# First rows, conversion steps and merge places reordered in a delta-rule, gated-MLP and Mish-MLP kernel

## The chip, the cores and the metric

One core of a Trainium2 chip. The metric is the time of one execution on the device in microseconds; the compiled program is fully unrolled, and each engine works through its own queue of instructions in the order in which the program issues them.

## The reference, cut to what matters

```python
B, H, S, D = 4, 8, 768, 48
k_n = k / (norm(k) + 1e-06)
for t in range(S):                                  # delta rule, state 48 x 48 for each of 32 heads
    y[:, :, t] = q_t @ state
    v_old = k_t @ state
    state = state + beta_t * outer(k_t, v_t - v_old)
x = y as 3072 tokens x 384
xn = x / sqrt(mean(x * x) + 1e-06) * rms_g          # first MLP, d_ff 1536
x = (silu(xn @ w_gate) * (xn @ w_val)) @ w_out
h = x @ w_in                                        # second MLP, d_ff 2048
out = (h * tanh(softplus(h))) @ w_out2
```

q, k, v, beta, x are float32; the weights come as float64 and are used as a high and a low part.

## The kernel before

The sequence is cut into 12 rows of 64 tokens, two to a segment. Within a row the delta rule becomes matrix products: the Gram matrix of k is turned into the inverse of a triangular 64 x 64 matrix (tile `A`, called Y when done), then values, outputs and the new state follow. The state goes from row to row, so the rows stand in a chain.

**Phase b1** (to about 482 us) works off the rows. `chain_row(r)` yields the stages of a row in an order written out by hand: `R0` for row 0, `R1` for row 1, `ROW` for the others. A letter is a stage: r residual of v against the state, q0 q1 turns (transposes) of q, p scores (masked Gram matrix), y output of the state, v values, o0 o1 outputs, k update of the state, s0 s1 x0 x1 normalisation and x for the MLP, and for row r+4: nA norm, nB scaling of k (on GpSimd), c0 c1 turns of k, g its Gram matrix. S, T, X, Y are s0, s1, x0, x1 of the row before, done late.

The inverses come in two kinds. `inlane(sg)` inverts all 32 x 32 blocks of a segment's two rows on VectorE (copies of products `pr`, sums, three 32 x 32 transposes, the last of them `yc`, L605), then ScalarE copies into `A` (L607 to L609). `merges(sg)` joins the 32 x 32 blocks of each row to 64 x 64 with TensorE (L621, L631) and ScalarE copies between. For the first two rows `quick_lane(r)` (VectorE, 16 x 16) and `quick_products(r)` (TensorE, L735, then the same merge) stand in. `lanes()` runs `inlane` of segment 2, 3, ... and, once a given share of it is issued, the merges of the segment before.

Beside the chain run: `part_a`, the first MLP for two of its six column pairs (due units by row in `DUE`, for row 1 behind a delay `OFF`); `cv`, the conversion of weights from float64 (`convs`); warm-up matmuls (`warm`). `merge(*streams)` interleaves them: of the (generator, weight) pairs it always takes the next step of the one with the smallest share of its weight done. So a weight says over which stretch of the row a stream's steps are spread, and a stream whose steps sum to more than its weight ends after the others. `PRE` writes out the turns (t), products (g), norms (n), scalings (s), warm-ups (w) and steps of row 0's chain (c) that are issued ahead of the rows.

`convs` takes half a weight tile at a time through: load into `raw` (ring of 4), absolute value into `t` (ring of 3; ScalarE L138, or VectorE L140), two steps of two VectorE instructions (L143, L146; L151, L154), and at last the high part (ScalarE L165, or VectorE L167) and the low part (GpSimd L168). The absolute value of the next half is issued ahead of the steps of this one.

**Phase b2** does the other four pairs of the first MLP, **phase c** the second MLP; both are block after block of matmuls. The last ten halves of `w_out2` (tiles `wqh`, `wql`) are converted at the end of b2 and in the first three batches of c, there with VectorE for every step but the low part.

At the start `setup` issues on SyncE the loads of k for rows 0 to 3, then beta for the quick inverses (`load_bq`, eight small loads for each of the first two row pairs), q, beta again, v, weights. Pools: `il` is closed when row 10 begins and its place is reused for converted weights, `kp` lives to the end of the rows.

Of the kernel before, what the change touches and what calls it, by code (L numbers as in the profile page):

```python
# [8 lines left out]
F32 = mybir.dt.float32  # L9
# [10 lines left out]
P = dict(  # L20
    XB=2, WE=16, RB=4, TB=3, LANE=15.7, XL=1, HH=0, DPRE=5, WU0=24, WU1=35, WARM=[0, 0], CVS=[2.6, 10.0, 2.5, 13.1, 0], CVA=12, CVT=12.22, CVB0=0, CVB1=1.238, CVC=2.31, PSD=1, INV=1, Q=[0, 2.7, 1.2, 9.9, 0, 18.8, 2.8, 3.0, 11.5, 10.6, 11.0, 19.4], W=[22, 2, 14, 8, 0, 14], SQ=5, CVP=0, NE=2, BQ=3, NU=6, CVN=1, CVE=14.671, CVD=4.076, OFF=2.9,
    ROW="r nA q0 q1 S p T y nB X Y v c0 c1 k o0 g o1".split(),
    R0="r q0 q1 p nA v o0 o1 s0 nB k s1 x0 c0 c1 g".split(),
    R1="r nA q0 Y q1 y p nB v k o0 o1 s0 s1 x0 c0 c1 g".split(),
    DUE=[0, 4, 6, 11],
    PRE="t00 t01 w1 g0 s1 n2 w2 s2 t10 | n3 t11 c g1 c c s3 t20 t21 | t30 g2 t31 w3 g3".split(),
    C=dict(n=0.2, q=0.5, r=1.4, y=1.1, p=1.2, v=1.2, o=0.9, k=1.2, s=0.1, x=0.45, c=0.4, d=0.4, g=1.2, h=1.2),
# [40 lines left out]
def kernel(  # L68
# [14 lines left out]
    nc = tc.nc  # L83
# [88 lines left out]
    def convs(pairs, wait=0):  # L172
        depth = P["RB"]
        gens = [g for p in pairs for g in p]
        for g in gens[:depth]:
            next(g)
        yield 0.1
        yield from delay(wait)
        next(gens[0])
        yield 0.2  # L180
        for i, g in enumerate(gens):
            if i + 1 < len(gens):
                next(gens[i + 1])
            for _ in range(2):
                next(g)
                yield 0.7
            if i + depth < len(gens):
                next(gens[i + depth])
            for _ in g:
                pass  # L190
            yield 0.1

    def cols(w, m):
# [82 lines left out]
    def phase_b1():  # L276
# [75 lines left out]
        def setup():  # L352
# [9 lines left out]
            for r in range(4):  # L362
                load_k(r)
                nc.vector.memset(khp[r][:, :, D:64], 0.0)
                if r == P["BQ"]:
                    load_bq(0)
                    load_q(0)
            load_bq(1)
            nc.gpsimd.memset(half, HALF)
# [143 lines left out]
        def inlane(sg):  # L513
# [85 lines left out]
            yield 1.1  # L599
            X11 = il.tile([128, 32, 32], F32, tag="X11", name="X11")  # L600
            nc.vector.transpose(out=X11.rearrange("p u r -> p r u"), in_=Nv.rearrange("p c r -> p r c"))
# [40 lines left out]
        def quick_lane(r):  # L642
# [7 lines left out]
            us = slice(r * 16, r * 16 + 16)  # L650
            compq = il.tile([128, 32, 32], F32, tag="X11", name="compq")
            comp = compq[:, 0:16, :]
# [110 lines left out]
        def merges(sg):  # L763
            X11 = X11_t.pop(sg)
            for rl in range(2):
                us = slice(rl * 16, rl * 16 + 16)
                Z = il.tile([128, 16, 32], F32, tag="Z", name="Z")
                yield from merge32(2 * sg + rl, X11[:, us], Z)

        def lanes():  # L770

            ending = iter(())
            for sg in range(2, NSEG):
                done_of, due = 0.0, 4.0
                for w in inlane(sg):
                    yield w
                    done_of += w
                    if done_of >= due:
                        next(ending, None)
                        due += 2.5  # L780
                for _ in ending:
                    pass
                ending = merges(sg)
            yield from delay(P["INV"])
            yield from ending

# [236 lines left out]
        sq = [flat(t)[:, 0:16 * D].rearrange("p (u d) -> p u d", d=D) for t in sq]  # L1023
        run(warm(W_[0]), norm(0), scale_k(0, nc.vector), norm(1, spare))
        chain0 = chain_row(0)
# [20 lines left out]
        for x in P["PRE"]:  # L1046
            if x == "|" or not PRE:
                PRE.append([])
            if x != "|":
                PRE[-1].append(x)  # L1050
        run(ahead_of(PRE[0]))
        merge((quick_lane(0), 12), (seq(delay(Q[0]), ahead_of(PRE[1])), Q[1] + Q[0]))

        def reset():
# [7 lines left out]
            (first, 7.0),  # L1062
            (quick_lane(1), Q[3]),
            (seq(delay(Q[4]), ahead_of(PRE[2])), Q[4] + Q[5]),
            (budget(cv, Q[6]), Q[7]),
        )
        lane, laned = lanes(), [0.0]
        M1A = 4.0 * FA + KD
        ps_ds = [ps_d]
        part_a = gated((ps_u, ps_ds, hp, tp), range(FA), range(NR), get_xa, finish_a, next_x)  # L1070
        for sg in range(NSEG):
            for rl in range(2):
# [10 lines left out]
                if r == 0:  # L1083
                    lane1 = seq(reset(), inlane(1), delay(P["INV"]), merges(1))
                    streams.append((budget(lane1, Q[8]), Q[8]))
# [3 lines left out]
                elif sg + 1 < NSEG:  # L1089
                    upto = (r - 1) * P["LANE"] if r < NR - 3 else 999.0  # L1090
                    streams.append((until(lane, laned, upto), P["LANE"] + (0.0 if r < NR - 3 else 7.0)))
                elif rl == 0:
                    st_i.close()
                    wbp.append(st_b.enter_context(pool("wbA")))
                    todo = [(c, m, cols(w, m)) for m in range(FA, NP1) for c, w in (("g", w_gate), ("v", w_val))]
# [190 lines left out]
```

## Time and profile before

| | us |
|---|---|
| runs (3) | 1235.88, 1236.47, 1233.67; median 1235.88 |
| the profiled execution | 1236.43 |
| its span, first to last instruction | 1234.7 |
| TensorE busy, matmuls | 1123.7 (91%) |
| VectorE busy | 732.4 (59%) |
| ScalarE busy | 561.9 (46%) |
| GpSimd busy | 438.2 (35%) |

The page shows in 40 slices of some 31 us that TensorE is at 90% and more from slice 17 on but for one dip, and at 40 to 90% before, with a granted clock of 0.6 to 0.8 in the first five slices. A busy share over the whole span therefore says little; the stretches below are read one by one. In these views PE is TensorE, DVE VectorE, ACT ScalarE, POOL GpSimd, SP SyncE; a q behind the name is the engine's own queue (DMA issues). In the order of time, a line gives start, duration, engine, line, operation, output and inputs, and in brackets the idle time before it and who ended it.

### The profile page before, as it was taken

What the parts mean: (1) busy time and instruction counts of PE and PEld (TensorE: products, weight loads), DVE (VectorE), ACT (ScalarE), POOL (GpSimd) and SP (SyncE); (2) the same over time, 40 slices, a digit from 0 to 9 for tenths busy, and PEclk for the clock granted to TensorE, in tenths of its full rate; (3) what the DMA queues carried; (4) which work ended last, traced back from release to release, by engine and by line L of the source; (5) the groups of instructions that cost most, each with busy time, mean ns of one, the idle gap of its engine ahead of it and who ended that gap; (6) DMA issues with size and microseconds to landing.
All of it is one profiled execution on the core that took longest, in us unless ns stands there. A gap on an engine that the chain in (4) does not pass through costs nothing.

```text
span 1234.7 us, 32507 instructions
## 1 busy us (share of the span) xinstructions
PE 1123.7 (91%) x14172; PEld 1092.3 (88%) x14172; DVE 732.4 (59%) x1135; ACT 561.9 (46%) x1064; POOL 438.2 (35%) x392
## 2 busy tenths in 40 slices
PE   6674598999997978999999999988999999999998
PEld 5563587989897868999999999987999999999998
DVE  5768697988886797555555552368434333343333
ACT  3463545656555654211111110154756555565672
POOL 2124244444421354344443442244323232232232
PEclk8667688999998899999999999999999999999999
DMA  6224032332223544333433222331111011111101
GB/s 121 52 67 104 14 79 68 78 84 75 70 77 104 143 142 154 116 103 122 135 115 105 90 82 98 124 103 56 39 39 40 22 31 39 40 40 39 34 7 26
DMA packets 121695, 95.02 MB, mean 77 GB/s; under 512 B 81104, under 2 KB 104144, under 8 KB 121552
## 3 DMA queue, kind: packets, MB, share of 16 engines
q1 hardware_dynamic: 109456, 69.34, 20.6%
q10 hardware_dynamic: 12096, 23.60, 5.7%
q8 instruction: 111, 1.82, 0.6%
q14 instruction: 32, 0.26, 0.1%
HBM read 64.60 MB, written 28.31 MB: 75 GB/s over the span
## 4 chain that ended last, share of the span: by engine, by line
PE 66%; DVE 16%; ACT 5%; issue 3%; POOL 1%; DMA 0%; DVEq 0%; POOLq 0%; ACTq 0%
PE pd L1182 5%; PE pd L1183 5%; PE pd L1181 5%; PE ph L210 5%; PE ph L211 5%; PE ph L212 5%; DVE pr L540 4%; PE pg L210 4%; PE pv L210 3%; PE pd L227 3%; PE pg L211 3%; PE pv L211 3%; PE pv L212 3%; PE pg L212 3%; PE pd L228 3%; PE pd L229 3%
## 5 line engine op out<-in xcount | busy, mean ns | idle before, releaser
L1229 POOL TENSOR_TENSOR gl<-t,gh 128x512 fp32r<-128x512 f32 x96 | 125.3, 1306 | 254.5 <-DVE gh L1228 253.1
L255 POOL TENSOR_TENSOR hl<-sg,hh 128x512 fp32r<-128x512 f32 x72 | 97.2, 1350 | 237.4 <-DVE hh L254 216.9
L210 PE MATMUL ph<-xh,wih 128*128 128x256 f32 x576 | 162.7, 283 | 4.6 <-DVE t L1225 4.6
L211 PE MATMUL ph<-xl,wih 128*128 128x256 f32 x576 | 162.7, 282 | 0.0
L212 PE MATMUL ph<-xh,wil 128*128 128x256 f32 x576 | 162.5, 282 | 0.0
L245 ACT ACTIVATE sg<-pg 128x512 f32<-128x512 f32 x72 | 43.0, 597 | 236.4 <-PE pg L212 206.8
L1181 PE MATMUL pd<-wqh,gh 128*128 128x384 f32 x384 | 130.3, 339 | 1.9 <-DVE wqh L167 1.9
L1182 PE MATMUL pd<-wql,gh 128*128 128x384 f32 x384 | 130.3, 339 | 1.7 <-POOL wql L168 1.7
L1183 PE MATMUL pd<-wqh,gl 128*128 128x384 f32 x384 | 129.9, 338 | 0.0
L211 PE MATMUL pg<-xl,wgh 128*128 128x256 f32 x432 | 124.2, 288 | 5.2 <-POOL xl L933 5.2
L210 PE MATMUL pg<-xh,wgh 128*128 128x256 f32 x432 | 128.3, 297 | 0.0
L210 PE MATMUL pv<-xh,wvh 128*128 128x256 f32 x432 | 127.7, 296 | 0.0
L227 PE MATMUL pd<-hh,woh 128*128 128x256 f32 x432 | 125.1, 290 | 2.2 <-DVE hh L254 1.6
L212 PE MATMUL pg<-xh,wgl 128*128 128x256 f32 x432 | 124.0, 287 | 0.0
L211 PE MATMUL pv<-xl,wvh 128*128 128x256 f32 x432 | 123.9, 287 | 0.0
L212 PE MATMUL pv<-xh,wvl 128*128 128x256 f32 x432 | 123.7, 286 | 0.0
L228 PE MATMUL pd<-hl,woh 128*128 128x256 f32 x432 | 122.4, 283 | 1.0 <-POOL hl L255 1.0
L229 PE MATMUL pd<-hh,wol 128*128 128x256 f32 x432 | 122.1, 283 | 0.0
L251 DVE TENSOR_TENSOR sg<-sg,pv 128x512 f32<-128x512 f32 x72 | 49.3, 685 | 112.9 <-PE pv L212 110.6
L1225 DVE TENSOR_TENSOR t<-t,ph 128x512 f32<-128x512 f32 x96 | 65.2, 680 | 83.5 <-ACT t L1223 83.4
L210 PEld LDWEIGHTS ph<-xh,wih 128*128 128x128 f32 x576 | 109.8, 191 | 4.8 <-DVE t L1225 4.8
L212 PEld LDWEIGHTS ph<-xh,wil 128*128 128x128 f32 x576 | 109.8, 191 | 0.0
(187 smaller groups left out, 2938.5 us busy)
## 6 DMA issues: line engine op xcount, KB each, us to landing
raw<-in_moe_w_out_dram SPq DMA_DIRECT2D x28, 384.0 KB
raw<-in_moe_w_in_dram SPq DMA_DIRECT2D x16, 384.0 KB
kh<-in_k_dram SPq DMA_DIRECT2D x24, 192.0 KB
qp<-in_q_dram SPq DMA_DIRECT2D x24, 192.0 KB
v<-in_v_dram SPq DMA_DIRECT2D x48, 96.0 KB
raw<-in_moe_w_gate_dram SPq DMA_DIRECT2D x12, 384.0 KB
raw<-in_moe_w_val_dram SPq DMA_DIRECT2D x12, 384.0 KB
xh_d<-xh SPq DMA_DIRECT2D x12, 384.0 KB
```

What stands on the lines that cost most here:

```text
L210: nc.tensor.matmul(ps[:, f, :], wh[:, kt, sl], xh[:, kt, :], start=(kt == 0), stop=False)
L211: nc.tensor.matmul(ps[:, f, :], wh[:, kt, sl], xl[:, kt, :], start=False, stop=False)
L212: nc.tensor.matmul(ps[:, f, :], wl[:, kt, sl], xh[:, kt, :], start=False, stop=(kt == KD - 1))
L227: nc.tensor.matmul(ps, wh[:, f, sl], hh[:, f, :], start=(i + f == 0), stop=False)
L228: nc.tensor.matmul(ps, wh[:, f, sl], hl[:, f, :], start=False, stop=False)
L229: nc.tensor.matmul(ps, wl[:, f, sl], hh[:, f, :], start=False, stop=last)
L255: nc.gpsimd.tensor_tensor(out=hl, in0=sg, in1=hh.bitcast(F32), op=ALU.subtract)
L1181: nc.tensor.matmul(ps, gh[:, f, sl], wh[:, f, :], start=(m + f == 0), stop=False)
L1182: nc.tensor.matmul(ps, gh[:, f, sl], wl[:, f, :], start=False, stop=False)
L1183: nc.tensor.matmul(ps, gl[:, f, sl], wh[:, f, :], start=False, stop=last)
L1225: nc.vector.tensor_tensor(out=t, in0=t, in1=ps, op=ALU.mult)
L1229: nc.gpsimd.tensor_tensor(out=gl, in0=t, in1=gh.bitcast(F32), op=ALU.subtract)
```

## The change

- Start: beta for the first pair of rows is loaded second (behind k of row 0), q third, beta again behind k of row 2. The scaling of k for row 1 is issued with its norm, the turns and products of row 0 at once behind it; turns of row 1 and row 0's chain steps beside lane 0, closed by 40 warm-ups; norms and scalings of rows 2 and 3 ahead of lane 1; turns and products of rows 2 and 3 in the later part of that merge.
- Orders: row 0 updates the state ahead of its outputs. From row 2 on nB stands ahead of y, v ahead of Y, k ahead of the turns of row r+4, and g last. Row 1 has 5 units of part_a instead of 4, behind a delay of 6 instead of 2.9; row 2 has 5 instead of 6.
- Merges: those of segment 1 (rows 2 and 3) go from the end of row 1's stream into `lanes`, beside the inverse of segment 2; within an inverse merges start at 2.5 units and follow every 2.0 (4.0 and 2.5 before). The last merges (rows 10 and 11) go from the end of row 9's lane into a stream of their own beside row 10. The lane is held 1.5 units behind.
- Conversions: the last step of a half (high and low part) is issued after the VectorE steps of the next half.
- The tiles `X11` (with `compq`) and `Z` move from pool `il` to `kp`.

```diff
-    ... W=[22, 2, 14, 8, 0, 14], ... OFF=2.9,
-    ROW="r nA q0 q1 S p T y nB X Y v c0 c1 k o0 g o1".split(),
-    R0="r q0 q1 p nA v o0 o1 s0 nB k s1 x0 c0 c1 g".split(),
+    ... W=[22, 40], ... OFF=6.0,
+    ROW="r nA q0 q1 S p T nB y X v Y k c0 o0 c1 o1 g".split(),
+    R0="r q0 q1 p nA v k o0 o1 s0 nB s1 x0 c0 c1 g".split(),
-    DUE=[0, 4, 6, 11],
-    PRE="t00 t01 w1 g0 s1 n2 w2 s2 t10 | n3 t11 c g1 c c s3 t20 t21 | t30 g2 t31 w3 g3".split(),
+    DUE=[0, 5, 5, 11],
+    PRE="t10 t11 c g1 c c w1 | t20 t21 g2 t30 t31 g3".split(),
...
+        last = iter(())
         for i, g in enumerate(gens):
             if i + 1 < len(gens):
                 next(gens[i + 1])
...
             if i + depth < len(gens):
                 next(gens[i + depth])
-            for _ in g:
+            for _ in last:
                 pass
+            last = g
             yield 0.1
+        for _ in last:
+            pass
...
-                if r == P["BQ"]:
+                if r == 0:
                     load_bq(0)
+                elif r == 1:
                     load_q(0)
-            load_bq(1)
+                elif r == 2:
+                    load_bq(1)
...
-            X11 = il.tile([128, 32, 32], F32, tag="X11", name="X11")
+            X11 = kp.tile([128, 32, 32], F32, tag="X11", name="X11")
...
-        def lanes():
-            ending = iter(())
+        def lanes(ending):
             for sg in range(2, NSEG):
-                done_of, due = 0.0, 4.0
+                done_of, due = 0.0, 2.5
...
-                        due += 2.5
+                        due += 2.0
...
-            yield from delay(P["INV"])
-            yield from ending
+            left.append(ending)
...
-        run(warm(W_[0]), norm(0), scale_k(0, nc.vector), norm(1, spare))
+        run(warm(W_[0]), norm(0), scale_k(0, nc.vector), norm(1, spare), scale_k(1))
...
-        run(ahead_of(PRE[0]))
-        merge((quick_lane(0), 12), (seq(delay(Q[0]), ahead_of(PRE[1])), Q[1] + Q[0]))
+        run(turn_k(0, 0), turn_k(0, 1), products(0))
+        merge((quick_lane(0), 12), (ahead_of(PRE[0]), 6.0))
...
             (first, 7.0),
-            (quick_lane(1), Q[3]),
-            (seq(delay(Q[4]), ahead_of(PRE[2])), Q[4] + Q[5]),
+            (seq(*[f(r, *a) for r in (2, 3) for f, a in ((norm, (sq[r - 2],)), (scale_k, ()))], quick_lane(1)), 12.5),
+            (seq(delay(8.0), ahead_of(PRE[1])), 14.0),
             (budget(cv, Q[6]), Q[7]),
...
-        lane, laned = lanes(), [0.0]
+        lane, laned, left = lanes(merges(1)), [0.0], []
...
-                    lane1 = seq(reset(), inlane(1), delay(P["INV"]), merges(1))
+                    lane1 = seq(reset(), inlane(1))
...
-                    upto = (r - 1) * P["LANE"] if r < NR - 3 else 999.0
-                    streams.append((until(lane, laned, upto), P["LANE"] + (0.0 if r < NR - 3 else 7.0)))
+                    upto = (r - 1) * P["LANE"] - 1.5 if r < NR - 3 else 999.0
+                    streams.append((until(lane, laned, upto), P["LANE"]))
                 elif rl == 0:
                     st_i.close()
+                    streams.append((seq(left.pop(), delay(7.0)), 13.0))
```

## Rows read from the trace of the kernel before

**Rows 1.** Busy time by stretch: us, length, busy of each engine, PEclk, DMA share, GB/s.
```profile
92.40:142.60 50.20, 24.21 (x480) 21.27 (x480) 45.92 (x61) 20.85 (x49) 22.95 (x17) 0.74 0.28 72
...
142.60:154.80 12.20, 7.96 (x257) 7.40 (x258) 0.04 (x1) 7.63 (x13) 0.18 (x1) 0.50 0.00 1
...
211.00:389.00 178.00, 167.34 (x3908) 155.81 (x3906) 153.13 (x195) 104.82 (x250) 67.42 (x59) 0.97 0.31 82
...
389.00:405.50 16.50, 12.81 (x291) 11.78 (x291) 1.23 (x4) 10.32 (x18) 2.00 (x3) 0.65 0.10 34
...
405.50:482.00 76.50, 64.41 (x955) 60.76 (x956) 62.71 (x100) 44.64 (x124) 36.94 (x38) 0.92 0.51 155
...
817.00:863.00 46.00, 37.68 (x250) 35.62 (x248) 43.21 (x70) 23.13 (x33) 22.86 (x19) 0.95 0.24 78
```

**Rows 2.** Who waited for whom on VectorE, 0 to 160 us: total, times, longest.
```profile
DVE v L818 <- PE pp L813: 18.9, 2, 12.2
...
DVE qc L646 <- DMA qc<-in_beta_dram: 5.9, 1, 5.9
...
DVE compq L509 <- ACT compq L508: 5.1, 1, 5.1
...
DVE PT L492 <- PE pp L483: 3.5, 1, 3.5
```

**Rows 3.** In order of time: SyncE's first loads and the first reader of k.
```profile
0.79 7.79 SPq L331 DMA_DIRECT2D kh<-in_k_dram  x8
...
5.53 0.84 ACT L423 ACTIVATE sq<-kh 128x768 f32<-128x768 f32 x1 [3.24 <-DMA kh<-in_k_dram]
...
8.63 6.17 SPq L358 DMA_DIRECT2D qc<-in_beta_dram  x8
...
16.25 5.77 SPq L358 DMA_DIRECT2D qc<-in_beta_dram  x8
```

**Rows 4.** In order of time: warm-ups, norm of k3 and lane 0's transpose.
```profile
12.75 3.39 PE L1013 MATMUL warm<-ident 128*128 128x128 f32 x28
...
24.23 0.95 DVE L425 TENSOR_REDUCE ss<-sq 128x16 f32<-128x768 f32 x1
...
26.46 1.04 DVE L659 STREAM_TRANSPOSE dq<-compq 128x512 f32<-128x512 f32 x1
```

**Rows 5.** In order of time: second and third product of row 0's inverse, TensorE.
```profile
41.03 1.54 PE L735 MATMUL pp<-Zq,YT 32*32 32x32 f32 x49 [1.42 <-DVE Zq L740]
...
51.56 1.10 PE L735 MATMUL pp<-YT,Zq 32*32 32x32 f32 x58
```

**Rows 6.** In order of time: end of segment 1's inverse, start of segment 2's.
```profile
139.67 1.92 DVE L605 STREAM_TRANSPOSE yc<-N__166 128x1024 f32<-128x1024 f32 x1
...
143.84 1.04 ACT L609 COPY A<-yc 32x1024 f32<-32x1024 f32 x1
...
155.70 1.28 DVE L509 SCALAR_TENSOR_TENSOR comp<-A,h,comp 128x1024 f32<-128x1024 f32 x1
```

**Rows 7.** Waits of TensorE, 0 to 500 us, and one of ScalarE's, whole span.
```profile
PE pp L502 <- POOL kh L449: 11.1, 4, 4.0
...
PE pp L899 <- ACT ve L855: 1.5, 6, 0.6
...
ACT wgh L165 <- DVE t L154: 15.5, 6, 3.8
```

**Rows 8.** In order of time: conversion steps in the dip, last product at its end.
```profile
824.98 0.35 DVE L140 TENSOR_SCALAR t<-raw 128x384 int32<-128x384 int32 x1
...
825.25 1.18 DVE L143 TENSOR_SCALAR t<-t 128x384 f32<-128x384 f32 x1
...
825.15 1.07 POOL L168 TENSOR_TENSOR wql<-t,wqh 128x384 fp32r<-128x384 f32 x1 [0.89 <-DVE wqh L167]
...
858.73 0.35 DVE L143 TENSOR_SCALAR t<-t 128x384 f32<-128x384 f32 x1
...
862.86 0.69 PE L1182 MATMUL pd<-wql,gh 128*128 128x384 f32 x1 [0.39 <-POOL wql L168]
```

More of the change, by code (lines that the diff above doesn't have):

```diff
@@ L20 @@
 P = dict(
-    XB=2, WE=16, RB=4, TB=3, LANE=15.7, XL=1, HH=0, DPRE=5, WU0=24, WU1=35, WARM=[0, 0], CVS=[2.6, 10.0, 2.5, 13.1, 0], CVA=12, CVT=12.22, CVB0=0, CVB1=1.238, CVC=2.31, PSD=1, INV=1, Q=[0, 2.7, 1.2, 9.9, 0, 18.8, 2.8, 3.0, 11.5, 10.6, 11.0, 19.4], W=[22, 2, 14, 8, 0, 14], SQ=5, CVP=0, NE=2, BQ=3, NU=6, CVN=1, CVE=14.671, CVD=4.076, OFF=2.9,
-    ROW="r nA q0 q1 S p T y nB X Y v c0 c1 k o0 g o1".split(),
-    R0="r q0 q1 p nA v o0 o1 s0 nB k s1 x0 c0 c1 g".split(),
+    XB=2, WE=16, RB=4, TB=3, LANE=15.7, XL=1, HH=0, DPRE=5, WU0=24, WU1=35, WARM=[0, 0], CVS=[2.6, 10.0, 2.5, 13.1, 0], CVA=12, CVT=12.22, CVB0=0, CVB1=1.238, CVC=2.31, PSD=1, INV=1, Q=[0, 2.7, 1.2, 9.9, 0, 18.8, 2.8, 3.0, 11.5, 10.6, 11.0, 19.4], W=[22, 40], SQ=5, CVP=0, NE=2, BQ=3, NU=6, CVN=1, CVE=14.671, CVD=4.076, OFF=6.0,
+    ROW="r nA q0 q1 S p T nB y X v Y k c0 o0 c1 o1 g".split(),
+    R0="r q0 q1 p nA v k o0 o1 s0 nB s1 x0 c0 c1 g".split(),
     R1="r nA q0 Y q1 y p nB v k o0 o1 s0 s1 x0 c0 c1 g".split(),
-    DUE=[0, 4, 6, 11],
-    PRE="t00 t01 w1 g0 s1 n2 w2 s2 t10 | n3 t11 c g1 c c s3 t20 t21 | t30 g2 t31 w3 g3".split(),
+    DUE=[0, 5, 5, 11],
+    PRE="t10 t11 c g1 c c w1 | t20 t21 g2 t30 t31 g3".split(),
     C=dict(n=0.2, q=0.5, r=1.4, y=1.1, p=1.2, v=1.2, o=0.9, k=1.2, s=0.1, x=0.45, c=0.4, d=0.4, g=1.2, h=1.2),
@@ L650, in quick_lane @@
             us = slice(r * 16, r * 16 + 16)
-            compq = il.tile([128, 32, 32], F32, tag="X11", name="compq")
+            compq = kp.tile([128, 32, 32], F32, tag="X11", name="compq")
             comp = compq[:, 0:16, :]
@@ L766, in merges @@
                 us = slice(rl * 16, rl * 16 + 16)
-                Z = il.tile([128, 16, 32], F32, tag="Z", name="Z")
+                Z = kp.tile([128, 16, 32], F32, tag="Z", name="Z")
                 yield from merge32(2 * sg + rl, X11[:, us], Z)
-        def lanes():
-            ending = iter(())
+        def lanes(ending):
             for sg in range(2, NSEG):
-                done_of, due = 0.0, 4.0
+                done_of, due = 0.0, 2.5
                 for w in inlane(sg):
```

## The prediction, made before the change was run

> **What bounds the kernel now.** I read the busy time by stretch first [rows 1], to see which engine is full where. From 482 us on TensorE runs almost without a break but for one dip, 817 to 863. Before 482 us it does not: 92.4 to 142.6 belongs to VectorE (45.92 of 50.2 us busy), 211 to 389 to both (TensorE 167.34 and VectorE 153.13 of 178 us). Two holes stand out: 142.6 to 154.8 (VectorE busy 0.04 us) and 389 to 405.5 (1.23 us). What ends late before 482 shifts all that follows, since the rest is TensorE work one behind the other; so a microsecond taken from the chain of the first stretch is a microsecond of the span, and one added in the dip too. Then I read who waited for whom on VectorE in the first 160 us [rows 2], and the order of time around each of those waits [rows 3 to 6].
>
> **Beta second.** The first 16-step inverse on VectorE waits 5.9 us for beta [rows 2]. SyncE issues eight loads of k in 7.79 us (0.97 each), eight beta loads in 6.17 and, after q, the last eight in 5.77, ending at 22.02 [rows 3]. The change puts one eight behind k0 and leaves only k3 (two issues, 1.9 us) behind the second. Beta comes 1.9 us sooner. k1 is moved behind the first eight: it is issued at 0.79 + 1.9 + 6.2 = 8.9 and, by the 4.7 us that k0 took from its issue to its reader at 5.53 [rows 3], arrives at 13.6. Its norm stands on ScalarE ahead of row 0's copies; with some 5 us for the norm (passes of 0.84 and 0.95 in [rows 3, 4]), copies and products these end near 18.5: later than before, but ahead of beta, whose issue alone ends at 22.02 - 1.9 = 20.1, so beta stays last.
> The Trainium skill speaks against this term: "DMA: Bandwidth & Descriptors", "Issuing engines are not separate DMA queues", calls a sequencer's issue time usually small relative to the DMA itself. Here it is not: 16 loads of 1 KB hold SyncE for 11.9 us [rows 3]. By the page the 1.9 us would be 0, and the time about 1217.
> The norm of k3, from 24.23 on VectorE, holds the transpose that starts the lane until 26.46 [rows 4]; put behind lane 0 it frees 2.2 us. Together 4.1 us at the end of lane 0. What is late next is TensorE: 40 warm-up matmuls now stand behind row 0's scores and ahead of the first product; at 0.12 us each (28 in 3.39 [rows 4]) 4.8 us, and double that at the lower clock level, which may take all 4.1 back. The two norms now ahead of lane 1 fall into the 5.1 us in which VectorE waited for compq [rows 2]. I take **-3.4**, between 0 and -4.1.
>
> **Row 0's products ahead of the turns.** The second product starts at 41.03, the third, which needs nothing newer than the second's operands, at 51.56 [rows 5]: between them TensorE's queue holds two turns, row 2's and row 3's products and warm-ups. In the new merge these start at 8 of 14, so row 0's inverse can end several us sooner, and its values, and row 1's inverse behind them. VectorE gains only where it waits: 18.9 - 12.2 = 6.7 us for row 1's residual and 3.5 us for row 1's scores [rows 2]. The second is TensorE standing in block 0's products ahead of the scores; their delay goes from 2 of 6.9 to 6 of 11 of the row, past the scores. Bounds 0 and -10.2; I take half, **-5**, because GpSimd's and ScalarE's queues hold both chains too.
>
> **Row 1 to row 2.** The inverse of rows 2 and 3 ends on VectorE at 139.67 + 1.92, its copies on ScalarE at 143.84 + 1.04 = 144.88 [rows 6]. Then both merges run, with nothing beside them, and only then row 2's residual and the next inverse, whose first VectorE step is at 155.70 [rows 6]. With the merges handed to the lane stream, that step needs only the copies and the diagonal on ScalarE, a pass as long as the last copy and taken at its 1.04: 145.9, so 9.8 us sooner. The merges do not vanish: this hole holds 7.96 us of TensorE at granted clock 0.50 [rows 1], 4.0 us at full speed, now inside row 2. If all of it lay on the path 5.8 would be left. Row 2 has 5 units of block work where later rows have 11, which leaves room: **-8**, bounds -5.8 and -9.8.
>
> **Rows 2 to 9, new order.** TensorE's largest wait is for GpSimd's scaled k, 11.1 us in four waits up to 4.0 [rows 7]. nB moves ahead of y and the turns behind Y and k, some three of a row's 12 cost units, so this wait should go. What comes instead: the state update now directly follows the values and their four ScalarE copies; that wait's longest is 0.6 now [rows 7], times eight rows +5. The moved nB puts a VectorE reciprocal sooner in its queue, behind it the inverse, and it may wait for GpSimd's power. TensorE idles only 10.7 us in the 178 [rows 1]: **-2**, between -8 and +5.
>
> **Row 9 to row 10.** The same hole, 16.5 us, with TensorE busy 12.81 at clock 0.65 [rows 1]: 8.3 us at full speed, so 8.2 can go. The last merges now run beside row 10's residual, turns and block work, and row 10's conversions find VectorE 10 us sooner. The merges' ping-pong with ScalarE still stands ahead of row 10's values: **-6**, bounds -2 and -8.2.
>
> **Conversions a half later.** ScalarE's cast no longer waits for VectorE (one tile's row of four: 15.5 us [rows 7]), but the next half's first step now follows at once on the low part that GpSimd has just been given, since three t tiles serve in a ring. In rows 10 and 11 the one against the other: **-1**, between -4 and +4 of the 12.1 us that TensorE idles there [rows 1].
> In the dip it costs. There the conversions run on VectorE alone, 43.21 of 46 us busy [rows 1], and the last product waits for the last low part at 862.86 [rows 8]. Now L143 of the next half takes 1.18 beside L168 and 0.35 alone [rows 8]: VectorE already loses 0.83 a half to GpSimd, ending at 826.43. After, L140 starts when L168 is done (826.22 + 0.1), then L140 and L143 at 0.35 each, ends overlapping by 0.1: 826.9. That is 0.5 for each of the seven halves that reuse a tile, 3.5; at the end two low parts come back to back, 1.07 [rows 8] and 0.3: **+4.9**. Behind the waiting L140 stand the half's four steps and the next batch's multiply, for which TensorE waits. Bounds: +1.4 (the end alone) and 7 x 1.25 + 1.4 = +10.2, if L143 stays at 1.18.
> The Trainium skill ("SBUF — State Buffer", "SBUF: two separate sides") has VectorE and GpSimd lock each other out for a whole instruction. By it the 0.83 is a wait for that same low part and is not paid twice, as the 0.35 row has it; were it no lock, the dip would cost the +10.2 and the time be 1221.
> The tiles moved to the longer-lived pool are the same instructions on other addresses: 0, as long as no new tile waits for theirs.
>
> **The sum.** -3.4 - 5 - 8 - 2 - 6 - 1 + 4.9 = -20.5. The profiled execution took 1236.43 (span 1234.7), 0.55 above the median of the runs, 1235.88: 1215.4, so 1215.
>
> **Rivals.**
> *The holes only move* (15%): row 2's and row 10's values wait for their merges as before, the queues in order stand still behind them, and the -8 and -6 go, -2 with them. Left: -3.4 - 5 - 1 + 4.9 = -4.5, 1231. For it: values stand in the middle of the row, the merges just before. Against: VectorE's next inverse needs no merge.
> *More than the sum* (12%): VectorE keeps full from lane 1 on (-10.2 for the -5) and the waits for scaled k go (-8): -32, 1204. For it: all these waits are on full engines. Against: each has a second wait close behind.
> *Slower: the ring of three t tiles* (11%). Each ScalarE half, 12 in rows 0 to 3 and 24 from row 10 to past the end of row 11, puts the absolute value behind a low part of 1.07 us, and behind what else GpSimd has queued, on the queue that also copies every transposed and merged tile. If all 36 reach the path that is +39, less the sum: 1254. It decides from 19 halves on, 19 x 1.07 = 20.3, about where the gain is used up; at 28 halves, +30, 1245. Against: ScalarE loses more to VectorE now, and the low part usually has a step of another stream ahead of the next half.
> *It does not do what it says* (beta still last at the same time, or copies of row 0 later than beta) costs at most the 3.4, and lies inside the forecast's own range.
>
> **How the numbers follow.** The forecast has 62%, own range 1208 to 1224. Reaching towards the rivals until 2 in 10 are left out, and over the bounds of the dip and of the new row order: 1203 to 1232. About 0.2%, 2.5 us, is what a measurement of this kernel can tell from no change. The forecast and the larger gain are faster, of the moved holes about two thirds: 0.84; the rest of those same, 0.05; slower 0.11.
>
> **What would show it.** In the profile after: VectorE's wait for beta a good 2 us shorter or ended sooner; row 0's third product within some 4 us of the second; no VectorE wait of 12 us before row 2 nor of 15 before row 10; the waits for scaled k gone from TensorE's list; in the dip an L140 waiting about 1.2 us for each L168, L143 at 0.35, the dip 5 us longer. Wrong would be: ScalarE's absolute value waiting for GpSimd for tens of us in the rows, merges with long waits on either side in rows 2 and 10, or a row pitch above the present one in rows 3 to 9.

## The result, and the profile after

The changed kernel takes 1221.12 us (median; 1220.54 to 1223.12), beside 1236.14 for the kernel before: a ratio of 0.9886, with a 95% interval of 0.9868 to 0.9903. Its profiled execution took 1221.12 (span 1219.4), against 1236.43 (span 1234.7): 15.3 us less, where the sum of the forecast was 20.5 less (1215). The time lies in the range, the sign is right, and most terms are not what they were said to be.

The stretches that answer to [rows 1] (length, then busy time of PE, PEld, DVE, ACT and POOL, granted clock, DMA share and GB/s):

```profile
93.20:143.60 50.40, 29.82 (x515) 27.43 (x515) 43.00 (x59) 20.32 (x48) 21.98 (x17) 0.65 0.28 72
...
143.60:149.30 5.70, 0.14 (x2) 0.00 (x0) 2.06 (x6) 5.47 (x7) 1.00 (x1) 0.70 0.35 69
...
204.00:376.70 172.70, 167.15 (x4013) 156.22 (x4011) 149.85 (x197) 107.62 (x256) 68.30 (x60) 1.00 0.33 87
...
376.70:392.90 16.20, 14.26 (x366) 13.39 (x366) 11.07 (x20) 11.33 (x22) 2.29 (x2) 0.79 0.30 75
...
392.90:467.00 74.10, 56.96 (x767) 53.90 (x767) 46.86 (x79) 39.57 (x110) 33.93 (x36) 0.86 0.47 145
...
801.50:849.80 48.30, 39.48 (x247) 37.75 (x246) 37.37 (x71) 23.18 (x33) 23.57 (x20) 0.89 0.23 74
```

The hole of 12.2 us between the inverse of rows 2 and 3 and the next is 5.7 long, and ScalarE fills it. The hole of 16.5 us ahead of row 10 is gone as a hole (VectorE 11.07 busy, where it had 1.23). But the first stretch is as long as it was. The last two of phase b1 don't begin at the same stage: 405.5 of [rows 1] is the end of VectorE's wait for row 10's residual, 392.9 here is row 10's values. Taken between stages that both traces have, from row 10's values to phase b2's first addition, TensorE idles 20.3 of 117.8 us, where it was 14.2 of 107.0.

Where the 15.3 us come from is read off marks that both traces have, in order of time. Of before, besides the two in [rows 6], the last inverse's end, row 10's values and phase b2's first addition:

```profile
387.14 2.03 DVE L605 STREAM_TRANSPOSE yc<-N__166 128x1024 f32<-128x1024 f32 x1
...
419.49 1.24 PE L850 MATMUL pp<-v,A 64*64 64x48 f32 x64
...
526.45 0.41 DVE L1143 TENSOR_TENSOR par<-par,pd 128x256 f32<-128x256 f32 x1
```

Of after, the same five marks (the start of each line counts; an inverse's end is its last transpose):

```profile
141.72 2.03 DVE L611 STREAM_TRANSPOSE yc<-N__166 128x1024 f32<-128x1024 f32 x1
...
149.26 1.28 DVE L515 SCALAR_TENSOR_TENSOR comp<-A,h,comp 128x1024 f32<-128x1024 f32 x1 [3.60 <-ACT comp L514]
...
372.46 1.94 DVE L611 STREAM_TRANSPOSE yc<-N__166 128x1024 f32<-128x1024 f32 x1
...
392.92 1.32 PE L854 MATMUL pp<-v,A 64*64 64x48 f32 x64
...
510.73 0.41 DVE L1148 TENSOR_TENSOR par<-par,pd 128x256 f32<-128x256 f32 x1
```

| from mark to mark | before | after | difference | forecast (its terms) |
|---|---|---|---|---|
| start to end of segment 1's inverse | 139.67 | 141.72 | +2.0 | -8.4 (beta second -3.4, row 0's products -5) |
| to the first step of segment 2's inverse | 16.03 | 7.54 | -8.5 | -8 (row 1 to row 2) |
| to the end of segment 5's inverse | 231.44 | 223.20 | -8.2 | -2 (rows 2 to 9) |
| to row 10's values | 32.35 | 20.46 | -11.9 | -6 (row 9 to 10) |
| to phase b2's first addition | 106.96 | 117.81 | +10.9 | -1 (conversions in rows 10 and 11) |
| to the end of the span | 708.25 | 708.67 | +0.4 | +4.9 (the dip) |

The two stretches that lost have one thing in common. In row 1, ScalarE, GpSimd, TensorE and VectorE of the kernel after, in order of time (one view for each engine, 84 to 124 us):

```profile
100.05 4.52 POOL L444 TENSOR_TENSOR nr<-ss,half 128x16 f32<-128x16 f32 x1 [6.00 <-DVE ss L431]
...
106.26 1.00 POOL L168 TENSOR_TENSOR wvl<-t,wvh 128x384 fp32r<-128x384 f32 x1
...
107.29 0.54 ACT L138 ACTIVATE t<-raw 128x384 f32<-128x384 f32 x1 [10.89 <-POOL wvl L168]
...
109.24 0.62 ACT L509 COPY QT<-pp 128x512 f32<-128x512 f32 x1
...
109.91 1.10 PE L835 MATMUL pp<-sx,QT 64*64 64x48 f32 x32 [13.19 <-ACT QT L509]
...
112.80 1.29 DVE L498 TENSOR_TENSOR PT<-pp,mpos 128x512 f32<-128x512 f32 x2 [4.18 <-PE pp L489]
```

To be read from the top: GpSimd's power for a norm (L444) stands ahead of a conversion's low part (L168). GpSimd itself waits 6.00 us for VectorE's sum of squares before the power can start at 100.05; the power takes 4.52 us, an addition behind it 1.53, the low part 1.00. ScalarE's absolute value for a later half (L138) needs the t tile that this low part reads and stands still for 10.89 us: some 3.6 of that is GpSimd's wait for VectorE, the rest what GpSimd then does; behind it the copy of q's turn (L509); TensorE waits for that copy 13.19 us, and VectorE for TensorE's scores 4.18. In rows 10 and 11 the same wait comes in small pieces, ScalarE from 400 to 500 us (total, times, longest):

```profile
ACT t L138 <- POOL wvl L168: 11.0, 6, 3.9
...
ACT t L138 <- POOL wgl L168: 10.6, 6, 3.1
...
ACT t L138 <- POOL wol L168: 9.6, 5, 4.1
```

31.2 us in 17 waits; in the same window of before this wait came once, with 0.4. That is the mechanism of the forecast's slower rival, inside a kernel that is faster all the same.

### The profile page after: what moved, and what is told of

It is laid out like the page before. It is cut to its first block, busy times and chain, and to the rows that moved or that the text cites. A ratio compares the mean times of both kernels' runs of the same rounds, so it can differ in the third digit from the quotient of the medians.

```text
span 1219.4 us, 32572 instructions
## 1 busy us (share of the span) xinstructions
PE 1117.9 (92%) x14204; PEld 1088.7 (89%) x14204; DVE 716.0 (59%) x1135; ACT 564.2 (46%) x1064; POOL 436.8 (36%) x392
## 4 chain that ended last, share of the span: by engine, by line
PE 69%; DVE 15%; ACT 6%; POOL 4%; issue 3%; SPq 1%; DMA 1%; DVEq 0%; POOLq 0%; ACTq 0%
PE pd L1187 5%; PE pd L1188 5%; PE pd L1186 5%; PE ph L216 5%; PE ph L214 5%; PE ph L215 5%; PE pd L231 4%; PE pd L232 3%; PE pd L233 3%; PE pv L214 3%; PE pg L214 3%; PE pv L215 3%; PE pv L216 3%; PE pg L216 3%; PE pg L215 3%
```

## The experiments

Each median stands beside runs of the kernel before on the same chip, and its ratio to those is given with a 95% interval. "Now" means a conversion's last step right behind its half, as before the change.

**The delay, and the ring it needs.** Theory A: the ring of three t tiles is where the two lost stretches come from. Theory B, on record: the delay gains a little in the rows and costs 4.9 in the dip.

```diff
 conv_now: the changed kernel, delay undone
-            for _ in last:
+            for _ in g:
                 pass
-            last = g
```

> The kernel after, with one part undone: every conversion's last step (cast and low part) stands right behind its half again, not a half later. Theory on record: the delay gains 1 us in the rows and costs 4.9 in the dip of phase c, so without it 1221.1 + 1 - 4.9 = 1217.2. Rival A, the ring of three t tiles in the rows: the trace after has ScalarE's absolute value waiting 10.9 us for GpSimd's low part in row 1 (VectorE's wait of 4.2 us for row 1's scores behind it) and 14.0 and 17.4 us in rows 10 and 11, while the first output of phase c moved by no more than the others: without the delay 4.2 in row 1 and some 6 in rows 10 and 11 come back, the dip gives 0.4: about 1210.5. Rival B, the delay pays in the rows (ScalarE's cast waits for VectorE again): 1223 or more.

1208.05 us, ratio 0.9784 (0.9769 to 0.9798): 13.1 less than the kernel after. The end of segment 1's inverse is at 136.15 (after: 141.72), row 10's values to the first addition take 110.5 (117.8). ScalarE's waits from 400 to 500 us without the delay:

```profile
ACT woh L165 <- DVE t L154: 11.0, 7, 2.7
...
ACT wvh L165 <- DVE t L154: 8.4, 4, 3.3
...
ACT t L138 <- POOL wgl L168: 0.4, 1, 0.4
```

The cast (L165) waits for VectorE as it did before the change, 29.2 us with the two lines not shown; the low part is waited for once. These waits are about as long together as the 31.2 that replaced them, and cost less; what makes the one sort of wait dearer than the other, no run took apart. Rival A holds, and its price was even low.

```diff
 dip_now: the delay undone in the last conversions alone (phase c's dip)
-        cv = convs([prepare(lambda: wbp[0], ("q", m), ...) for m in range(QE, NP2)])
+        cv = convs([prepare(lambda: wbp[0], ("q", m), ...) for m in range(QE, NP2)], lag=False)
```

> The kernel after, with the delay undone in the last conversions alone (the tiles converted on VectorE without ScalarE, from the end of phase b2 into the dip of phase c). Theory on record: the dip's 4.9 us come back, 1216.2. Rival A (and B): the product blocks behind the dip have slack for a later last tile, only the 0.4 us by which the last output moved less than the blocks ahead of the dip comes back: 1220.7.

1219.14 us, ratio 0.9877 (0.9862 to 0.9892), which can't be told from after's 0.9886. The 4.9 us are not there. In the kernel after the dip shows just what the forecast drew, in order of time VectorE and GpSimd (seven such L140):

```profile
810.37 0.36 DVE L140 TENSOR_SCALAR t<-raw 128x384 int32<-128x384 int32 x1 [1.13 <-POOL wql L168]
...
810.64 0.35 DVE L143 TENSOR_SCALAR t<-t 128x384 f32<-128x384 f32 x1
...
813.98 0.36 DVE L140 TENSOR_SCALAR t<-raw 128x384 int32<-128x384 int32 x1 [1.13 <-POOL wql L168]
...
847.76 2.02 POOL L168 TENSOR_TENSOR wql<-t,wqh 128x384 fp32r<-128x384 f32 x2 [1.75 <-DVE wqh L167]
```

L140 waits 1.13 for the low part, L143 takes 0.35, two low parts come back to back at the end. But from one L140 to the next it is 3.61 (813.98 - 810.37), where before it was 3.35 (824.98, which is in [rows 8], to 828.33): 0.26 more and not 0.5. The first output of phase c comes 13.4 us sooner than before where the b2 addition came 15.7 sooner: 2.3 lost, and the second block's first output is 15.7 sooner again. What gave the 2.3 back is TensorE's clock. The end of the dip and the block behind it, of before:

```profile
860.00:868.30 8.30, 6.73 (x24) 6.01 (x25) 4.59 (x10) 0.00 (x0) 1.78 (x2) 0.60 0.17 38
...
863.90:903.20 39.30, 39.30 (x267) 39.30 (x267) 14.98 (x22) 23.17 (x33) 11.64 (x9) 0.94 0.11 31
```

Of after:

```profile
844.00:852.50 8.50, 6.80 (x31) 6.16 (x32) 5.34 (x12) 0.00 (x0) 3.06 (x3) 0.80 0.02 5
...
850.50:887.50 37.00, 37.00 (x266) 37.00 (x265) 15.05 (x21) 23.19 (x33) 11.67 (x9) 1.00 0.12 33
```

And with the dip's delay undone:

```profile
843.00:851.20 8.20, 6.63 (x25) 5.91 (x26) 4.50 (x9) 0.00 (x0) 1.84 (x2) 0.58 0.18 41
...
846.75:885.90 39.15, 39.15 (x267) 39.15 (x267) 14.96 (x22) 23.16 (x33) 11.62 (x9) 0.94 0.11 31
```

From the first to the fourth output TensorE is busy without a break in all three. Before, it enters this stretch at the lower level and takes 39.3 us for it; after, the clock is at full again by then, and it takes 37.0; with the delay undone it is 39.15 again.

```diff
 ring4_raw3: the changed kernel with the delay and a wider ring
-    XB=2, WE=16, RB=4, TB=3, ...
+    XB=2, WE=16, RB=3, TB=4, ...
```

> The kernel after with four t tiles in the conversions' ring and three tiles for the raw loads (there is no room for four of both): the delay stays, but the next half's first step no longer needs the tile of the half whose low part has just been given out. Theory on record: in the dip the waits of L140 go, 3.5 of the 4.9 us, in the rows nothing: 1217.6. Rival A, the ring in the rows: ScalarE's waits for GpSimd's low part shrink to near nothing, and 4.2 us in row 1 and some 6 in rows 10 and 11 come back: 1211, unless the raw loads, started a half later, take part of it. Rival B: 1221, as after.

1204.26 us, ratio 0.9746 (0.9728 to 0.9765): 16.9 less than after and 3.8 less than without the delay. From 400 to 500 us ScalarE's L138 now waits for its raw load (14.6 us in three lines, 7.2 the largest) and hardly for the low part:

```profile
ACT t L138 <- DMA raw<-in_moe_w_out_dram: 7.2, 4, 3.1
...
ACT t L138 <- POOL wgl L168: 3.0, 2, 2.3
```

The wide ring might be a gain of its own. So conv_now with the same ring:

```diff
 now_ring4: conv_now with the wider ring
-    XB=2, WE=16, RB=4, TB=3, ...
+    XB=2, WE=16, RB=3, TB=4, ...
```

> The kernel after without the conversions' delay and with four t tiles and three raw tiles. Tells whether the wide ring only undoes what the delay costs or lets the delay pay. If the delay is worth nothing in itself: as the kernel with both, 1204. If it pays once the ring is wide enough (ScalarE's cast waited 42.5 us for VectorE without it): as without the delay and three tiles, 1208. If the raw ring of three costs: over 1208.

1208.58 us, ratio 0.9784 (0.9770 to 0.9797): the ring alone is worth nothing, and the delay pays 4 us on it. And the delay alone on the kernel before:

```diff
 before_lag: the kernel before
-            for _ in g:
+            for _ in last:
                 pass
+            last = g
```

> The kernel before with the delay of the conversions alone. Theory on record: -1 in the rows and +4.9 in the dip on 1236.1: 1240. Rival A: the ring in the rows costs it 4 to 10 us and the dip 0.4: 1241 to 1246. Rival B, the delay pays in the rows: 1234 or less.

1244.18 us, ratio 1.0080 (1.0063 to 1.0096): it makes the kernel before 9.7 us slower. Taken together, the delay costs 10 to 13 us in a ring of three and gains 4 in one of four.

**The other parts, taken back one by one** from the kernel without the delay (1208.05), so that the ring doesn't cover them.

```diff
 c_merges_old (cut)
-                    lane1 = seq(reset(), inlane(1))
+                    lane1 = seq(reset(), inlane(1), delay(P["INV"]), merges(1))
-                    upto = (r - 1) * P["LANE"] - 1.5 if r < NR - 3 else 999.0
+                    upto = (r - 1) * P["LANE"] if r < NR - 3 else 999.0
-                    streams.append((seq(left.pop(), delay(7.0)), 13.0))
```

> The kernel without the conversions' delay (1208.05), with the last merges of each pair of rows put back: behind the inverse at the end of row 1 and of row 9 with nothing beside them, and the lane's old due times. Theory on record: the two holes cost 8 and 6 us again: 1222. Rival, the holes only move: 1208 to 1210. The trace of the kernel without the delay has row 10's values 32.9 us sooner than before where row 9's are 28.0 sooner, so 4.9 for the second hole.

1232.65 us, ratio 0.9983 (0.9966 to 1.0001), 24.6 more by the medians; its profiled execution, 1228.16, is the fastest of its nine, 21.1 over that without the delay. By the marks of the two traces: +10.5 from the end of segment 1's inverse to that of segment 2's and +5.6 from the last inverse to row 10's values, so some 16 for the two holes, where the forecast had 14; the rest, +5.1, lies in the rows between, where the merges' old due times are.

```diff
 c_row_old
-    ROW="r nA q0 q1 S p T nB y X v Y k c0 o0 c1 o1 g".split(),
+    ROW="r nA q0 q1 S p T y nB X Y v c0 c1 k o0 g o1".split(),
```

> The kernel without the conversions' delay (1208.05), with the old order of stages in rows 2 to 11. Theory on record: the new order is worth 2 us: 1210. Rival from the traces: the eight rows 2 to 9 each lost a microsecond of TensorE's wait for the scaled k, the bound of 8 on record: 1216. If the new order only moved a wait: 1208.

1220.82 us, ratio 0.9884 (0.9865 to 0.9903): the order is worth 12.8, more than either side had. By the marks 6.8 us of it come before row 4: from the end of segment 1's inverse to that of segment 2's it is 65.4 us with the old order and 58.6 with the new, and VectorE waits 7.8 us there for state updates (new order: 1.5) and TensorE 4.5 for a scaled k (new: none). Another 6.8 come from there to the end of segment 5's inverse, and some 2.5 are given back in rows 10 and 11. From the end of segment 2's inverse to that of segment 5, the stretch in the four kernels, before, old merges, old order, neither old:

```profile
207.50:387.10 179.60, 168.94 (x3983) 157.22 (x3977) 153.31 (x196) 107.57 (x256) 68.93 (x61) 0.97 0.31 79
```

```profile
204.90:381.20 176.30, 164.86 (x3913) 154.12 (x3905) 151.60 (x196) 105.29 (x250) 71.83 (x59) 0.97 0.29 76
```

```profile
203.50:381.50 178.00, 169.55 (x4021) 157.93 (x4017) 150.45 (x198) 107.56 (x259) 69.72 (x63) 0.99 0.32 85
```

```profile
194.70:365.90 171.20, 167.12 (x4018) 156.41 (x4016) 150.14 (x199) 108.01 (x257) 68.14 (x62) 1.00 0.33 88
```

The new order alone takes 3.3 us off these 179.6, the new due times of the merges alone 1.6, both 8.4. Each is read from one trace, but this stretch hardly moves from run to run: it is 171.1 to 172.0 in all ten kernels that have both. TensorE's waits go with it: with the old order the scaled k is waited for either way (4.6 and 5.2 us), with the old due times TensorE idles 11.4 us and its clock is 0.97; with both it idles 4.1 of 171.2 at full clock. From before and from the old order, TensorE's wait for the scaled k:

```profile
PE pp L502 <- POOL kh L449: 4.6, 2, 2.6
```

```profile
PE pp L505 <- POOL kh L452: 5.2, 2, 2.6
```

```diff
 c_start_old (cut): the old start
-                if r == 0:
+                if r == P["BQ"]:
                     load_bq(0)
...
-    W=[22, 40]
+    W=[22, 2, 14, 8, 0, 14]
...
-        run(turn_k(0, 0), turn_k(0, 1), products(0))
-        merge((quick_lane(0), 12), (ahead_of(PRE[0]), 6.0))
+        run(ahead_of(PRE[0]))
+        merge((quick_lane(0), 12), (seq(delay(Q[0]), ahead_of(PRE[1])), Q[1] + Q[0]))
```

> The kernel without the conversions' delay (1208.05), with the old start: old order of the loads, old places of the norms, old order of row 0's products, the turns, the warm-ups (2, 14 and 8 in place of 40) and block 0's products. Theory on record: beta second and row 0's products ahead of the turns are worth 3.4 + 5 = 8.4: 1216.5. Rival from the trace: the end of the inverse of rows 2 and 3 stands only 3.5 us sooner than before in the kernel without the delay (136.2 against 139.7), so 1211.5. If VectorE was full anyway: 1208.

1206.68 us, ratio 0.9766 (0.9744 to 0.9789), not to be told from 0.9784. (The edit also takes back row 0's order of stages and the block units of rows 1 and 2.) In the traces the end of segment 1's inverse comes 3.7 us later with the old start (139.8 against 136.15), and the profiled executions differ by 2.5; but of their four runs each, the one is the slowest with the old start and the other the fastest without the delay. So a gain from the whole new start is not shown at the end of the kernel; 3.7 us at the mark is the most that can be claimed. Why not 8.4 is in the order of time of TensorE, VectorE and ScalarE of the kernel after:

```profile
20.66 0.39 DVE L652 TENSOR_SCALAR qc<-qc 128x32 f32<-128x32 f32 x2 [4.37 <-DMA qc<-in_beta_dram]
...
26.56 9.20 PE L1017 MATMUL warm<-ident 128*128 128x128 f32 x80
...
31.79 1.10 DVE L716 STREAM_TRANSPOSE Yd<-e 128x512 f32<-128x512 f32 x1
...
35.69 1.43 PE L741 MATMUL pp<-Yd,off 32*32 32x32 f32 x128
...
39.11 1.05 PE L741 MATMUL pp<-YT,Zq 32*32 32x32 f32 x55
...
41.42 0.95 DVE L431 TENSOR_REDUCE ss<-sq 128x16 f32<-128x768 f32 x1 [3.38 <-ACT sq L429]
...
46.82 0.22 ACT L435 ACTIVATE rt<-ss 128x16 f32<-128x16 f32 x1 [2.58 <-DVE ss L431]
...
49.13 1.05 DVE L665 STREAM_TRANSPOSE dq<-compq 128x512 f32<-128x512 f32 x1
...
49.65 1.17 ACT L631 COPY Z<-pp 32x512 f32<-32x512 f32 x2
...
52.05 1.92 PE L741 MATMUL pp<-YT,Zq 32*32 32x32 f32 x64 [5.16 <-ACT A L765]
...
58.02 1.20 PE L637 MATMUL pp<-A,Z 32*32 32x32 f32 x64
```

Beta is used at 20.66 (23.3 before). The 40 warm-ups are 80 records and hold TensorE for 9.20 us, to 35.69, where the operand of row 0's first product is ready at 32.9 (L716). Then the third product stands right behind the second (39.1, was 51.56 in [rows 5]), but VectorE takes up the first of the two norms only at 41.42, after 3.4 us of waiting for its square, and the second lane's transpose starts at 49.13 (before: 46.88). The fourth product is at 52.05 (before: 57.81): it waits 5.16 us for ScalarE's copies (L631, then L765), and these stand in ScalarE's queue behind the square root of the second norm (L435) and the second lane's first steps. Row 0's merge, behind the turns, is at 58.02, where it was 59.34 before.

```diff
 r_warm8: ring4_raw3 with fewer warm-ups
-    W=[22, 40]
+    W=[22, 8]
```

> The kernel after with four t tiles and three raw tiles (1204.26), with 8 warm-up products ahead of row 0's first in place of 40. The trace after has these 40 on TensorE for 9.2 us, to 35.69, where the operand of the first product is ready at 32.9: theory, the 2.8 us come back in row 0 and go on through VectorE's inverse of rows 2 and 3: 1201.5. Rival 1, VectorE's conversions and norms stand ahead of the second lane all the same: 1204. Rival 2, the granted clock of row 0's products falls without them, and the time is 1206 or more.

1200.45 us, ratio 0.9723 (0.9704 to 0.9743): 3.8 less by the medians, 2.8 by the ratios, whose intervals overlap a little. Segment 1's inverse ends at 133.8 (with 40: 137.6), 3.7 sooner, and the two profiled executions differ by 4.3. Eight warm-ups are gone long before the operand comes:

```profile
25.41 2.05 PE L1017 MATMUL warm<-ident 128*128 128x128 f32 x16
...
32.60 1.93 PE L741 MATMUL pp<-Yd,off 32*32 32x32 f32 x128 [5.14 <-DVE Yd L716]
```

Row 0's first product now starts 3.1 us sooner, though it runs at the lower clock level (granted clock 0.50 in its stretch, 1.00 behind 40), 1.93 us in place of 1.43.

```diff
 rw_sq: r_warm8 with the squares of k2 and k3 ahead of and beside the first lane
-        run(turn_k(0, 0), turn_k(0, 1), products(0))
-        merge((quick_lane(0), 12), (ahead_of(PRE[0]), 6.0))
+        run(turn_k(0, 0), turn_k(0, 1), products(0), square(2, sq[0]))
+        merge((quick_lane(0), 12), (seq(ahead_of(PRE[0]), square(3, sq[1])), 6.0))
```

> The kernel with four t tiles and 8 warm-ups (1200.45), in which ScalarE squares k2 and k3 ahead of and beside the first lane; the rest of their norms stays ahead of the second lane. Theory: of the step on record that the two norms fall into VectorE's wait of 5.1 us, only the sums do not hold: in the trace VectorE waits 4.1 us for the first square, which stands on ScalarE behind a copy that waits for TensorE, and the second lane's transpose starts later than before (47.6 against 46.9). With the squares early it starts some 4 us sooner and the inverse of rows 2 and 3, on a full VectorE, ends as much sooner: 1196.5. Rival, the values of row 0 and what follows hang on TensorE's queue in row 0, not on the second lane: 1200.

1199.55 us, ratio 0.9714 (0.9699 to 0.9730), within the measurement of 1200.45. The second lane starts 1.7 us sooner (45.91 against 47.58) and row 0's values 2.0, but segment 1's inverse ends at 133.7 as before it (133.8): the rival holds. The norm's square root on ScalarE, behind the same copy, took over part of the wait (VectorE 2.6), and VectorE's wait for row 1's residual grew from 4.9 to 5.9.

```diff
 rw_beta_old: r_warm8 with the old order of the loads
-                if r == 0:
+                if r == P["BQ"]:
                     load_bq(0)
-                elif r == 1:
                     load_q(0)
-                elif r == 2:
-                    load_bq(1)
+            load_bq(1)
```

> The kernel with four t tiles and 8 warm-ups (1200.45), with the old order of the first loads. Theory on record: beta comes 1.9 us later: 1202.3. If the first lane's start does not reach the end: 1200.5. If k1, whose norm now stands ahead of row 0's copies, was what the new order made late: 1199.

1203.66 us, ratio 0.9748 (0.9734 to 0.9761), 3.2 more by the medians, with intervals that overlap a little; the inverse of segment 1 ends at 137.4, 3.6 later. Row 10's values come 3.2 later (387.33 against 384.15), phase b2's first addition only 0.8, and the two profiled executions take the same (1200.90 and 1201.01). So the order of the loads is worth 3 to 4 us to the end of row 9; how much of it reaches the end of the kernel, 0 or some 3, these runs leave open.

```diff
 rw_sq_w28: rw_sq with more warm-ups
-    W=[22, 8]
+    W=[22, 28]
```

> The kernel with four t tiles and the early squares (1199.55), with 28 warm-ups in place of 8. In the traces 40 warm-ups take 9.2 us (0.23 each) and hold TensorE 2.8 us past the operand of row 0's first product; 8 leave it idle for 5.1 us, and that product then takes 1.93 us where it took 1.43 behind 40. 28 should end just ahead of the operand. If only the hold costs and the shorter products of row 0 help: 1198 to 1199. If the products of row 0 are off the path: 1199.5. If 28 hold them too: 1201 or more.

1200.01 us, ratio 0.9737 (0.9715 to 0.9760); not told apart from 8. What the warmer start of row 0 gives doesn't reach the end.

The best versions are r_warm8 and rw_sq, 1200.45 and 1199.55: the change with a ring of four t tiles and eight warm-ups, some 21 us below the kernel after and 35 below the kernel before.

## Why the prediction was right, and where it was not

**Beta second** (-3.4): beta came 2.6 us sooner, and the order of the loads alone is worth 3.6 at the end of segment 1's inverse and 3.2 in the medians (rw_beta_old, with the reserve said there). The two groups of eight loads are beta of row 0 and of row 1, not of row pairs; the first inverse waits for both, because its first step takes beta of both rows at once (`bq`, L646). The issue of eight loads of 1 KB holds SyncE 5.87 us in the trace of after too, and in both traces the first reader starts 1.3 us behind the end of the last such issue. The Trainium skill's sentence that the time to initiate a DMA is usually small relative to the DMA itself ("DMA: Bandwidth & Descriptors", "Issuing engines are not separate DMA queues") would have had 0 here; these traces decide against it. The failed step is the price of the warm-ups. I read "28 in 3.39" [rows 4] as 28 instructions; each of these is two records, so they were 14, and 40 of them are 9.2 us and not 4.8. The prediction said that they might take all 4.1 back, and took -3.4 all the same. They took some 3.7 at the end of segment 1's inverse (r_warm8).

**The norms ahead of lane 1**: the sentence that they fall into VectorE's wait of 5.1 us [rows 2] counted VectorE's sums and not the ScalarE steps, which stand in a queue behind a copy of row 0. It moved lane 1 by 2.2 us the wrong way, but as rw_sq shows that did not set the end.

**Row 0's products ahead of the turns** (-5): the third product within some 4 us of the second is what came, 12 us sooner than before, and the gain did not go on to row 0's values: 1.8 us sooner (60.13 against 61.93), because the fourth product waits for ScalarE's copies behind the norms that this change put there, and the merge stands behind rows 2's and 3's turns. Without the delay row 0's values come at 60.02 with the new start and at 60.03 with the old. VectorE's wait of 6.7 for row 1's residual stayed 6.1. That for the scores grew from 3.5 to 4.2, through the ring: without the delay it is gone, and with the old start put back it is 3.9, about as much as segment 1's inverse then ends later. So of the two waits priced here, the scores' was the one to be had. With the wider ring and eight warm-ups the first stretch is 5.8 us shorter than before (133.8 against 139.67), of the two terms' 8.4; in the change as it stands two costs cover it: 5.6 for the ring (141.72 against 136.15) and 3.7 for the warm-ups. This mark moves by some 1 us by itself (140.63 in dip_now, which is the same kernel up to there).

**Row 1 to row 2** (-8): -8.5 by the marks; the merges found room in row 2, for from the next inverse's first step to its end it is 51.4 us, where it was 51.8. **Row 9 to row 10** (-6): 5.6 by the merges put back. The -11.9 at the mark holds more: row 9's values were 21.4 us sooner where the last inverse was 14.7 sooner, so rows run ahead of the lane. 3.6 of that is given back in rows 10 and 11 even without the delay.

**Rows 2 to 9** (-2, between -8 and +5): -8.2. The wait for the scaled k went, as said; the state update's wait for the copies of the values, priced at up to +5, did not come there (TensorE's L903 waits 2.7 us from 141 to 380 us, behind other steps of ScalarE; the wait of 3.7 for the copies is row 0's). What the sum could not have is that the order and the merges' due times need each other: added one at a time they give 3.3 and 1.6, together 8.4 from row 4 on.

**Conversions in the rows** (-1, between -4 and +4): +13 by conv_now, the largest miss, and beyond its bounds. The mechanism stood in the text twice: as "the next half's first step now follows at once on the low part", and as the slower rival. What failed is the reason given against it, that the low part usually has another stream's step ahead of the next half. In rows 10 and 11 that held for two of 17 absolute values (392 to 470 us); the other 15 waited, 28.0 us. In row 1 GpSimd's queue was not free either: its wait of 6.00 us for VectorE's sum and its power of 4.52 us stood ahead, which the rival's price of 1.07 a half did not have. Up to 500 us ScalarE waited 54.7 us so, in 27 waits, and the kernel lost 13. The rival's +39, all on the path, was farther off than the -1.

**The dip** (+4.9): L140 waits and L143 at 0.35 as drawn, and +0.4 at the end. The pitch of a half grew by 0.26 and not 0.5. The Trainium skill ("SBUF — State Buffer", "SBUF: two separate sides") has a GpSimd instruction and a VectorE instruction of certain forms lock each other out for a whole instruction. By that the 0.83 is not paid twice; the rows agree, since with L143 still at 1.18 the pitch would by the prediction's sum have grown by 1.25 us. The 2.3 us that the dip had lost at its first output the block behind it gave back, by its clock; no term had the clock.

So the time was right by its range, and in part by luck: by the marks the start and the conversions came out 10.4 and 11.9 worse than forecast, rows 2 to 9, the last hole and the dip 6.2, 5.9 and 4.5 better, which nearly cancels. The mechanism of the holes held (-8 and -6), the term for rows 2 to 9 was too small, and those gains paid for the ring and the warm-ups, which the sum had at nearly nothing.

## What to carry to other kernels

A step that is put off by one stage of a pipeline keeps its buffer for one stage more: the ring wants one tile more, and without it the wait only changes its place, here to the queue that serves everything else. Before a duration from a row that counts records is multiplied, count by a known row how many records one instruction leaves. And where two edits clear two waits that end close to each other, their gains are not a sum: price the pair.

## What the runs showed of the hardware that was not expected

TensorE's clock came out differently behind two dips that look much alike. In the dip's last 10 us of before it waits 0.23, 0.68, 0.53, 0.68, 1.19 and 0.39 us for the last tiles, the last of them up to 862.86; its products then take 0.52 us (the granted clock from 860 to 868.3 is 0.60) and are at full level again from 868.4. After, the waits are three, 0.63, 1.90 and 0.68, the last up to 846.07, and products are back from 0.52 to 0.34 us at 849. That is 5.5 us at the lower level in the one and some 3 in the other, and the block behind takes 39.3 and 37.0 us for the same work. What the two differ in, beyond these waits, no run took apart.

And the clock did not decide where it seemed to: behind 40 warm-ups row 0's first product takes 1.43 us, behind 8 it takes 1.93, and the kernel with 8 ends segment 1's inverse 3.7 us sooner and is 3.8 us faster by the medians.
